# A second raw tile for layer 2's weight conversion, and one place more between the low parts and the products of batch 1's k-q tiles

## The chip, the core and the metric

The kernel runs on one core of one Trainium2 chip. The core has a matrix engine (TensorE, here PE; its weight loads are PEld), two engines for elementwise work and reductions (VectorE, DVE; ScalarE, ACT), a third, slower one (GpSimd, POOL), and SyncE (SP), which in this kernel issues every DMA from one queue in order. Each engine runs its own instructions in order and waits on semaphores for the others. The metric is the time of one execution in microseconds (us) on the device, lower is better.

## What is computed

Three stages follow one another. An attention over channels, with B = 2 batches of N = 6080 rows and C = 256 channels; then two feed-forward layers of width 2048 over the 12160 rows:

```python
qn = q / (np.linalg.norm(q, axis=1, keepdims=True) + 1e-06)
kn = k / (np.linalg.norm(k, axis=1, keepdims=True) + 1e-06)
s = kn.transpose(0, 2, 1) @ qn / tau             # [B, C, C]
a = softmax(s)                                    # over the last axis
x = (v @ a).reshape(12160, 256)

r = np.maximum(x @ w_in, 0.0)                     # layer 1
x = (s * (r * r) + b) @ w_out

h = x @ w2_in                                     # layer 2
x = (h * np.cos(h)) @ w2_out
```

q, k and v come in as float32 and the weights as float64; the kernel reads a float64 as two int32 words and makes a float32 of them itself.

## The kernel before

Every float32 operand of a matmul is split into a high part and a low part (`hi`, `lo`), and every product is three matmuls: high by high, high by low, low by high. The 12160 rows are cut into 12 pairs of blocks (512 columns, and 480 in the last pair of each batch). A **unit** is one pair against one of NJ = 8 slices of the 2048 hidden features; layer 1 is units 0 to 95 (NL = 96) and layer 2 units 96 to 191. From unit 8 on a unit forms its four hidden blocks with seven products instead of eight (a Strassen scheme), which is 21 matmuls of 512 columns at line 294, and then 24 output matmuls at line 419 for the unit before it.

The order of PE, ACT, DVE and POOL is written out by hand in the main loop. The order of a unit on PE is mm1 and mm5; **hook 0**; the first output block (6 matmuls); hook 1; mm6, mm2, the second output block; **hook 2**; mm7, mm3; **hook 4**; the third and fourth output block, mm4; **hook 6**; then hook 7 and the next unit. mm7 (line 294, into `ps_u` or `ps_x`) waits for `add6` (DVE, line 333), which reads what mm6 has written.

Side work is done in small steps that are hung on those hooks: `at(k, h, fn)` puts a function at hook h of unit k, and `steps(generators, places)` advances a generator by one `yield` at each place. A step's instructions stand in each engine's queue at that hook. Two pieces of side work are touched here.

**Batch 1's k-q tiles (`qk1`, lines 633 to 660).** While layer 1 works on batch 0 (units 9 to 38), 48 tiles of 128 rows of q and k are read, and their products are summed for batch 1's attention. The places are hooks 0, 2, 4 and 6 of 30 units, 120 in all. Tile i starts at the place `starts` gives it (line 846): there ACT makes the high parts `qk1h` (line 642) and the squares (line 648). At the next place DVE makes the low parts `qk1l` (line 652) and POOL adds the squares (line 654). At the place after that PE runs six matmuls of 256 columns (line 659), which read `qk1h` and `qk1l`. Both have two buffers, so the high part of tile i + 2 has to wait for the products of tile i.

**Layer 2's weights (`cv2_next`, lines 739 to 763).** From unit 50 on, sixteen blocks of layer 2's float64 weights are converted, alternating between a block `c` of the first matrix and a block `d` of the second (c0, d0, c1, d1, ...). One place is one of the hooks 0, 1, 6, 7. A `c` takes ten places and a `d` six, so that a pair takes four units: c0 and d0 start in units 50 and 52, c1 and d1 in 54 and 56, and so on to c7 and d7 in 78 and 80. A block's conversion (`conv`) reads the tile `raw` in its first three steps (ACT line 98, DVE lines 97, 100 and 103). In the block's fifth step the load of the next block into `raw` is issued (`cv2_load`, line 736). `raw` has one buffer. A `c` then ends in the tiles `ch` and `cl` (7 x 128 floats; ACT line 169, POOL line 171) and a `d` in `wh` and `wl` (2 x 256 floats; ACT line 760, DVE line 762), which `save` (line 455) writes to DRAM; layer 2 fetches them from there. Each of these four has one buffer of its own.

In units 48, 56, 64, 72 and 80, where layer 1 goes over to the next pair, hook 7 also issues the loads of the pair after it (`x_load`, line 249): sixteen DMAs into `xraw`, in the same SP queue as all else.

Of the kernel before, what the change touches and what calls it, by code (L numbers as in the profile page):

```python
# [10 lines left out]
F32R = mybir.dt.float32r  # L11
I32 = mybir.dt.int32
# [4 lines left out]
P = 128  # L17
# [23 lines left out]
def fused_kernel(ctx: ExitStack, tc: tile.TileContext, q, k, v, tau, w_in, w_out, ms, mb, w2_in, w2_out, res):  # L41
    nc = tc.nc
    act, dve, pe, sp, pool = nc.scalar, nc.vector, nc.tensor, nc.sync, nc.gpsimd
# [47 lines left out]
    def conv(raw, cp, res, nx=2):  # L91

        H, L = raw[:, :, :, 1], raw[:, :, :, 0]
        x = cp.tile([P, 2, 2 * P], I32, tag="cx", name="cx", bufs=nx)
        a = cp.tile([P, 2, 2 * P], F32, tag="ca", name="ca", bufs=1)
        f = x.bitcast(F32)
        dve.tensor_scalar(out=x, in0=H, scalar1=3, scalar2=0x3FFFFFFF, op0=ALU.logical_shift_left, op1=ALU.bitwise_and)  # L97
        act.activation(out=a, in_=H, func=AF.Abs)
        yield
        dve.scalar_tensor_tensor(out=x, in0=H, scalar=-(1 << 30), in1=x, op0=ALU.bitwise_and, op1=ALU.bitwise_or)  # L100
        act.activation(out=a, in_=a, func=AF.Abs, bias=-float(1 << 30))
        yield
        dve.scalar_tensor_tensor(out=x, in0=L, scalar=29, in1=x, op0=ALU.logical_shift_right, op1=ALU.bitwise_or)
        yield
        dve.scalar_tensor_tensor(out=f, in0=a, scalar=float(127 << 20), in1=f, op0=ALU.is_le, op1=ALU.mult)
        res.append(f)
        yield

    def in_src(w, j):
        return w[:, 4 * P * j:4 * P * (j + 1)].rearrange("(k p) (f t) -> p k f t", p=P, t=2)  # L110

    def out_src(w, j):
        return w[2 * P * j:2 * P * (j + 1), :].rearrange("(k p) (f t) -> p k f t", p=P, t=2)
# [47 lines left out]
    def combine(Af, hi, lo, o=0):  # L161

        for x, a, b, op in ((4, 0, 3, ALU.add), (6, 1, 0, ALU.subtract)):
            dve.tensor_tensor(out=Af[:, x, :], in0=Af[:, a, :], in1=Af[:, b, :], op=op)
        yield
        for x, a, b, op in ((5, 4, 1, ALU.subtract), (7, 2, 5, ALU.subtract)):
            dve.tensor_tensor(out=Af[:, x, :], in0=Af[:, a, :], in1=Af[:, b, :], op=op)
        yield
        act.copy(out=hi[:, o:7, :], in_=Af[:, 1 + o:8, :])
        yield  # L170
        pool.tensor_tensor(out=lo[:, o:7, :], in0=Af[:, 1 + o:8, :], in1=hi[:, o:7, :].bitcast(F32), op=ALU.subtract)
# [277 lines left out]
    def save(key, hi, lo):  # L449
        w = 1  # L450
        for x in hi.shape[1:]:
            w *= x
        t = dr.tile([2, P, w], F32, tag=f"kp{key[0]}{key[1]}", name="kept")
        for i, x in enumerate((hi, lo)):
            sp.dma_start(out=t[i], in_=x.rearrange("p a b -> p (a b)").bitcast(F32))
        keep[key] = t
# [50 lines left out]
    with tc.tile_pool(name="pro", bufs=2) as pro:  # L507
# [18 lines left out]
        for c, (t0, p, nj) in enumerate(chunks):  # L526
            rk, rq = raw_t.pop(c)
            hi = pro.tile([P, JM, 4, P], F32R, tag="qkh", name="qkh", bufs=HB)
            lo = pro.tile([P, JM, 4, P], F32R, tag="qkl", name="qkl", bufs=HB)
# [86 lines left out]
    nt1 = (N + P - 1) // P  # L616
# [12 lines left out]
    def qk1_load(i):  # L629
        p = st1["pool"]  # L630
        n = min(P, N - i * P)
        r = p.tile([P, 2, C], F32, tag="qk1", name="qk1", bufs=3)
        sp.dma_start(out=r[0:n, 0, :], in_=k[1, i * P:i * P + n, :])
        sp.dma_start(out=r[0:n, 1, :], in_=q[1, i * P:i * P + n, :])
        st1["r", i] = (r, n)

    def qk1(i):
        p = st1["pool"]
        r, n = st1.pop(("r", i))
        hi = p.tile([P, 2, C], F32R, tag="qk1h", name="qk1h", bufs=2)  # L640
        lo = p.tile([P, 2, C], F32R, tag="qk1l", name="qk1l", bufs=2)
        act.copy(out=hi[0:n], in_=r[0:n])
        acc, S = st1["acc"], st1["S"]
        if i == 0:
            act.activation(out=acc, in_=r, func=AF.Square)
        else:
            sq = p.tile([P, 2, C], F32, tag="sq1", name="sq1", bufs=1)
            act.activation(out=sq[0:n], in_=r[0:n], func=AF.Square)
        if i + 2 < nt1:
            qk1_load(i + 2)  # L650
        yield
        dve.tensor_tensor(out=lo[0:n], in0=r[0:n], in1=hi[0:n].bitcast(F32), op=ALU.subtract)
        if i:
            pool.tensor_tensor(out=acc[0:n], in0=acc[0:n], in1=sq[0:n], op=ALU.add)
        yield
        for m in range(2):
            ksl = slice(m * P, (m + 1) * P)
            for a, (w, x) in enumerate(((hi, hi), (hi, lo), (lo, hi))):
                pe.matmul(S[:, m * C:(m + 1) * C], lhsT=w[0:n, 0, ksl], rhs=x[0:n, 1, :],  # L659
                          start=(i == 0 and m == 0 and a == 0), stop=(i == nt1 - 1 and m == 1 and a == 2), skip_group_check=True)  # L660
# [64 lines left out]
    st2 = {}  # L725
    gst = ExitStack()
    cv2 = [x for j in range(NJ) for x in (("c", j, in_src(w2_in, j)), ("d", j, out_src(w2_out, j)))]

    def cv2_open():
        fst.close()  # L730
        st2["pool"] = gst.enter_context(tc.tile_pool(name="cv2", bufs=1, side="right"))
        cv2_load(0)

    def cv2_load(i):
        raw = st2["pool"].tile([P, 2, 2 * P, 2], I32, tag="raw", name="raw", bufs=1)
        sp.dma_start(out=raw, in_=cv2[i][2])
        st2[i] = raw

    def cv2_next(i):
        kind, j, _ = cv2[i]  # L740
        p = st2["pool"]
        res = []
        yield from conv(st2.pop(i), p, res, 1)
        x = res[0]
        if i + 1 < len(cv2):
            cv2_load(i + 1)
        if kind == "c":
            Af = afp.tile([P, 8, P], F32, tag="Af", name="Af", bufs=1)
            xv = x.rearrange("p k (f c) -> p k f c", f=2)
            for m, sl in ((0, slice(1, None, -1)), (1, slice(2, 4))):  # L750
                act.activation(out=Af[:, sl, :], in_=xv[:, m], func=AF.Copy, scale=INV_A)
            yield
            for m, sl in ((0, slice(1, None, -1)), (1, slice(2, 4))):
                dve.scalar_tensor_tensor(out=Af[:, sl, :], in0=xv[:, m], scalar=INV_B, in1=Af[:, sl, :], op0=ALU.mult, op1=ALU.add)
            yield
            hi, lo = [p.tile([P, 7, P], F32R, tag=f"c{h}", name=f"c{h}", bufs=1) for h in "hl"]
            yield from combine(Af, hi, lo)
        else:
            hi, lo = [p.tile([P, 2, 2 * P], F32R, tag=f"w{h}", name=f"w{h}", bufs=1) for h in "hl"]
            act.activation(out=hi, in_=x, func=AF.Copy, scale=TWO_PI)  # L760
            yield
            dve.scalar_tensor_tensor(out=lo, in0=x, scalar=TWO_PI, in1=hi.bitcast(F32), op0=ALU.mult, op1=ALU.subtract)
        save((kind, j), hi, lo)
# [70 lines left out]
    places = [(u, h) for u in range(NJ + 1, NU0 - NJ - 1) for h in (0, 2, 4, 6)]  # L834
    active = []

    def qk1_place(i):
        for g in list(active):
            if next(g, 0) == 0:
                active.remove(g)  # L840
        if i is not None:
            g = qk1(i)
            next(g)
            active.append(g)

    starts = {(len(places) - 4) * i // nt1: i for i in range(nt1)}
    for x, pl in enumerate(places):
        at(*pl, lambda i=starts.get(x): qk1_place(i))
    u = NU0 - NJ - 1
# [1 line left out]
    for j in range(NJ):  # L851
        steps([lazy(fold1, j)], [(NU0 - NJ + 1 + j, h) for h in (0, 1, 3, 4, 6, 7)])
    at(NU0 + 2, 0, cv2_open)
    todo = steps([lazy(cv2_next, i) for i in range(2 * NJ)],
                 [(u, h) for u in range(NU0 + 2, NL - 2) for h in (0, 1, 6, 7)][1:])

# [67 lines left out]
    for k_ in range(NJ, NU + 1):  # L924
        p, j = divmod(k_, NJ)
# [123 lines left out]
```

## Time and profile before

| | |
|---|---|
| median of three runs | 2157.35 us (2155.8 to 2158.29) |
| the profiled execution | 2159.99 us, its span 2158.2 us |
| PE busy | 2106.7 us, 98% of the span |
| PEld, DVE, ACT, POOL busy | 80%, 77%, 73%, 40% |
| mean granted clock of PE | 0.993 of full speed |
| HBM | 57 GB/s over the span |

The span is what lies between the first instruction and the last. Busy shares are means over stages. Most of the idle time of DVE, ACT and POOL is waiting for the others in a chain in which PE hardly ever stops, so the stretches in which PE itself stops are the ones to look for.

### The profile page before, as it was taken

The numbers are of one execution on the slowest core, as the hardware profiler recorded it, in microseconds if no ns is written. First come the engines' busy times: TensorE is split into PE (matmuls) and PEld (weight loads), VectorE is DVE, ScalarE is ACT, GpSimd is POOL, SyncE is SP. The second block draws the span as 40 slices with busy tenths as digits, with TensorE's granted clock in tenths as the row PEclk, the third lists the DMA queues.
The fourth block names the chain that finished last, engine by engine and source line by source line (L and its number), as shares of the span: only waits on it lengthen the run. The fifth ranks groups of instructions, "written<-read, shape, count | busy, mean of one in ns | idle before, by whom it ended". The sixth has DMA issues, their size and how long they took to land.

```text
span 2158.2 us, 28236 instructions
## 1 busy us (share of the span) xinstructions
PE 2106.7 (98%) x9478; PEld 1733.6 (80%) x9478; DVE 1664.8 (77%) x2410; ACT 1577.1 (73%) x2829; POOL 853.8 (40%) x638
## 2 busy tenths in 40 slices
PE   8799999999999999999999999999999999999997
PEld 7587888888788787878888888888888888888886
DVE  7787977777678787878666778778777777777775
ACT  7686766676666665756657888888888888888875
POOL 0003544443243332323223455444544554444544
PEclk9899999999999999999999999999999999999999
DMA  8432131230312313233053011011011011011011
GB/s 251 127 127 69 40 79 41 72 77 13 88 34 71 105 57 86 74 86 85 0 176 122 15 30 35 15 29 34 15 30 34 15 30 31 18 29 26 4 20 19
DMA packets 255523, 124.80 MB, mean 58 GB/s; under 512 B 206736, under 2 KB 221840, under 8 KB 255376
## 3 DMA queue, kind: packets, MB, share of 16 engines
q1 hardware_dynamic: 255376, 122.99, 21.4%
q8 instruction: 74, 1.21, 0.2%
q14 instruction: 73, 0.60, 0.1%
HBM read 82.31 MB, written 40.63 MB: 57 GB/s over the span
## 4 chain that ended last, share of the span: by engine, by line
PE 76%; DVE 6%; ACT 2%; DMA 1%; issue 1%; SPq 0%; POOL 0%; DVEq 0%; ACTq 0%; POOLq 0%
PE ps_y L419 39%; PE ps_s L294 20%; PE ps_u L294 11%; PE ps_x L294 4%; PE ps_x L659 1%; DVE d L380 1%; DVE r L375 1%; DVE gl L406 1%; DMA raw<-in_moe_w_in_dram 1%; DVE cx L97 1%; ACT gh L401 1%; PE ps_x L179 1%; ACT r L363 0%; DVE ps_s L333 0%; DVE d L349 0%
## 5 line engine op out<-in xcount | busy, mean ns | idle before, releaser
L406 POOL TENSOR_TENSOR gl<-r,gh 128x512 fp32r<-128x512 f32 (+1 forms) x560 | 730.1, 1311 | 1087.7 <-ACT gh L401 716.7
L419 PE MATMUL ps_y<-gh,WOh 128*128 128x512 f32 (+1 forms) x1536 | 474.0, 390 | 0.2 <-ACT gh L401 0.2
L419 PE MATMUL ps_y<-gl,WOh 128*128 128x512 f32 (+1 forms) x1536 | 472.3, 389 | 0.7 <-POOL gl L406 0.7
L419 PE MATMUL ps_y<-gh,WOl 128*128 128x512 f32 (+1 forms) x1536 | 472.5, 389 | 0.0
L401 ACT CAST gh<-r 128x512 fp32r<-128x512 f32 (+1 forms) x680 | 416.4, 616 | 7.0 <-DVE r L375 3.7
L419 PEld LDWEIGHTS ps_y<-gl,WOh 128*128 128x128 f32 x1536 | 288.1, 188 | 62.0 <-POOL gl L406 3.1
L419 PEld LDWEIGHTS ps_y<-gh,WOl 128*128 128x128 f32 x1536 | 288.6, 188 | 59.5
L419 PEld LDWEIGHTS ps_y<-gh,WOh 128*128 128x128 f32 x1536 | 286.9, 188 | 59.1 <-ACT gh L401 0.9
L294 PE MATMUL ps_s<-xh,WIh 128*128 128x512 f32 (+1 forms) x778 | 308.4, 396 | 1.1 <-DVE r L375 0.7
L294 PE MATMUL ps_s<-xh,WIl 128*128 128x512 f32 (+1 forms) x778 | 304.3, 391 | 0.6 <-DVE WIl L822 0.6
L294 PE MATMUL ps_s<-xl,WIh 128*128 128x512 f32 (+1 forms) x778 | 303.0, 390 | 0.0
L375 DVE TENSOR_TENSOR r<-r,ps_s 128x512 f32<-128x512 f32 (+1 forms) x374 | 251.5, 672 | 3.6 <-ACT r L363 2.7
L333 DVE TENSOR_TENSOR ps_s<-s,ps_u 128x512 f32<-128x512 f32 (+1 forms) x136 | 93.7, 689 | 198.1 <-ACT r L369 62.2
L396 ACT ACTIVATE r<-r 128x512 f32<-128x512 f32 (+1 forms) x384 | 228.8, 621 | 3.8 <-DVE r L390 3.8
L363 ACT ACTIVATE r<-ps_s 128x512 f32<-128x512 f32 (+1 forms) x197 | 116.7, 593 | 121.5 <-PE ps_s L294 121.1
L294 PEld LDWEIGHTS ps_s<-xh,WIh 128*128 128x128 f32 x778 | 146.5, 188 | 48.8 <-DVE r L375 21.0
L294 PE MATMUL ps_u<-xh,WIh 128*128 128x512 f32 (+1 forms) x431 | 170.3, 395 | 12.9 <-DVE ps_s L333 12.3
L385 ACT ACTIVATE n<-ps_s 128x512 int32<-128x512 f32 (+1 forms) x192 | 114.3, 595 | 84.0 <-PE ps_s L294 83.9
L294 PEld LDWEIGHTS ps_s<-xh,WIl 128*128 128x128 f32 x778 | 146.6, 188 | 31.9 <-DVE WIl L822 1.1
L294 PE MATMUL ps_u<-xl,WIh 128*128 128x512 f32 (+1 forms) x431 | 168.7, 391 | 0.0
L294 PE MATMUL ps_u<-xh,WIl 128*128 128x512 f32 (+1 forms) x431 | 168.4, 391 | 0.0
L294 PEld LDWEIGHTS ps_s<-xl,WIh 128*128 128x128 f32 x778 | 146.8, 189 | 26.2
(167 smaller groups left out, 3282.0 us busy)
## 6 DMA issues: line engine op xcount, KB each, us to landing
xraw<-in_v_dram SPq DMA_DIRECT2D x160, 64.0 KB, 2.6
ys<-dr SPq DMA_DIRECT2D x40, 256.0 KB, 2.5
xraw<-ys SPq DMA_DIRECT2D x40, 256.0 KB, 2.7
out_dram<-dr SPq DMA_DIRECT2D x160, 64.0 KB, 2.0
raw<-in_moe_w_in_dram SPq DMA_DIRECT2D x16, 512.0 KB, 3.7
raw<-in_moe_w_out_dram SPq DMA_DIRECT2D x16, 512.0 KB, 3.6
qk<-in_k_dram SPq DMA_DIRECT2D x47, 128.0 KB, 2.1
qk<-in_q_dram SPq DMA_DIRECT2D x47, 128.0 KB, 2.2
```

Source lines behind the costliest of these rows:

```text
L97: dve.tensor_scalar(out=x, in0=H, scalar1=3, scalar2=0x3FFFFFFF, op0=ALU.logical_shift_left, op1=ALU.bitwise_and)
L179: pe.matmul(pf[:, m * C:(m + 1) * C], lhsT=eT[a][:, e, m * P:(m + 1) * P], rhs=w[:, e, :], start=(n == 0), stop=(n == 5))
L294: pe.matmul(acc[:, 0:n], lhsT=a[:, w, :], rhs=b[:, 0:n], start=(start and s == 0), stop=(stop and s == 2), skip_group_check=True)
L333: dve.tensor_tensor(out=U[k_, "e"][:, 0:n], in0=U[k_, "s5"][:, 0:n], in1=U[k_, "b"][:, 0:n], op=ALU.add)
L363: act.activation(out=r[:, 0:n], in_=U[k_, i][:, 0:n], func=AF.Relu)
L375: dve.tensor_tensor(out=r[:, 0:n], in0=r[:, 0:n], in1=h[:, 0:n], op=ALU.mult)
L380: dve.scalar_tensor_tensor(out=h[:, 0:n], in0=h[:, 0:n], scalar=0.0, in1=h[:, 0:n], op0=ALU.max, op1=ALU.mult)
L385: act.activation(out=q_[:, 0:n], in_=U[k_, i][:, 0:n], func=AF.Copy, bias=0.25)
L396: act.activation(out=r[:, 0:n], in_=r[:, 0:n], func=AF.Sin, bias=HALF_PI, scale=TWO_PI)
L401: act.copy(out=G[k_, i][0][:, 0:n], in_=RR[k_, i][:, 0:n])
L406: eng.tensor_tensor(out=lo[:, 0:n], in0=RR.pop((k_, i))[:, 0:n], in1=hi[:, 0:n].bitcast(F32), op=ALU.subtract)
L419: pe.matmul(accs[p, t][m][:, 0:n], lhsT=wo[w][:, f, m * P:(m + 1) * P], rhs=g[x][:, 0:n], start=(j == 0 and f == 0 and s == 0), stop=(j == ...
```

## The change

```diff
@@ qk1
         if i:
             pool.tensor_tensor(out=acc[0:n], in0=acc[0:n], in1=sq[0:n], op=ALU.add)
         yield
+        yield
         for m in range(2):
@@ cv2_open, cv2_load
         cv2_load(0)
+        cv2_load(1)
 
     def cv2_load(i):
-        raw = st2["pool"].tile([P, 2, 2 * P, 2], I32, tag="raw", name="raw", bufs=1)
+        raw = st2["pool"].tile([P, 2, 2 * P, 2], I32, tag="raw", name="raw", bufs=2)
@@ cv2_next
-        if i + 1 < len(cv2):
-            cv2_load(i + 1)
+        if i + 2 < len(cv2):
+            cv2_load(i + 2)
@@ cv2_next, the branch of a block d
-            hi, lo = [p.tile([P, 2, 2 * P], F32R, tag=f"w{h}", name=f"w{h}", bufs=1) for h in "hl"]
+            hi, lo = [p.tile([P, 2, 2 * P], F32R, tag=f"c{h}", name=f"w{h}", bufs=1) for h in "hl"]
@@ where the places of qk1 are laid out
-    starts = {(len(places) - 4) * i // nt1: i for i in range(nt1)}
+    starts = {(len(places) - 5) * i // nt1: i for i in range(nt1)}
```

The products of a k-q tile move one place back, three places after the tile's start; the starts are spread over 115 places instead of 116. `raw` gets a second buffer, the first two blocks are loaded at the opening, and each block's step then loads the block two further on. In exchange `wh` and `wl` share the one buffer of `ch` and `cl` each (one tag names one set of buffers), which takes 4096 bytes less of each partition, as much as the second `raw` takes.

## Rows read from the trace of the kernel before

**Rows 1.** The page, part 1: busy us, share of the span, instructions.

```profile
PE 2106.7 (98%) x9478; PEld 1733.6 (80%) x9478; DVE 1664.8 (77%) x2410; ACT 1577.1 (73%) x2829; POOL 853.8 (40%) x638
```

**Rows 2.** The chain of work that ended last, by time: start us, us, what.

```profile
661.02 2.72 PE ps_y L419 x12
671.22 2.72 PE ps_y L419 x12
...
702.28 2.72 PE ps_y L419 x12
...
722.68 2.72 PE ps_y L419 x12
...
789.80 2.72 PE ps_y L419 x12
...
810.20 2.72 PE ps_y L419 x12
...
878.55 2.72 PE ps_y L419 x12
...
898.95 2.72 PE ps_y L419 x12
...
966.07 2.72 PE ps_y L419 x12
...
986.47 2.72 PE ps_y L419 x12
...
1007.46 2.72 PE ps_y L419 x12
```

**Rows 3.** Waits, 640 to 1010 us: who waited for whom, us in total, times, longest.

```profile
DVE cx L97 <- DMA raw<-in_moe_w_in_dram: 16.3, 3, 6.3
```

**Rows 4.** Instructions by time: start us, us, what, idle time before with its releaser.

```profile
664.75 0.38 DVE L97 TENSOR_SCALAR cx<-raw 128x512 int32<-128x512 int32 x1
...
754.45 0.43 DVE L97 TENSOR_SCALAR cx<-raw 128x512 int32<-128x512 int32 x1 [5.04 <-DMA raw<-in_moe_w_in_dram]
...
755.53 0.79 PE L294 MATMUL ps_u<-xh,WIh 128*128 128x512 f32 x1 [3.02 <-DVE ps_s L333]
```

**Rows 5.** The same view of SP's queue alone, 700 to 752 us.

```profile
700.04 0.38 SPq L736 DMA_DIRECT2D raw<-in_moe_w_in_dram  x1
...
738.08 0.32 SPq L455 DMA_DIRECT2D kept<-cl  x1
...
738.92 9.59 SPq L249 DMA_DIRECT2D xraw<-in_v_dram  x16
...
749.61 0.41 SPq L736 DMA_DIRECT2D raw<-in_moe_w_in_dram  x1
```

**Rows 6.** Stretches: from:to, length, busy us by engine, clock, DMA share, GB/s.

```profile
755.42:758.83 3.41, 3.29 (x8) 2.62 (x9) 2.30 (x5) 1.92 (x5) 0.00 (x0) 0.50 0.00 0
```

**Rows 7.** Waits, 200 to 530 us.

```profile
PEld ps_x L659 <- DVE qk1l L652: 3.8, 7, 1.4
...
PE ps_x L659 <- DVE qk1l L652: 1.7, 2, 1.0
```

**Rows 8.** Instructions by time, 236 to 239 us, of POOL, DVE and PE.

```profile
236.41 1.73 POOL L654 TENSOR_TENSOR acc1s<-acc1s,sq 128x512 f32<-128x512 f32 x1
...
236.93 1.77 DVE L652 TENSOR_TENSOR qk1l<-qk,qk1h 128x512 fp32r<-128x512 f32 x1
...
237.42 0.28 PE L659 MATMUL ps_x<-qk1h 128*128 128x256 f32 x1
...
238.75 0.39 PE L659 MATMUL ps_x<-qk1l,qk1h 128*128 128x256 f32 x1 [1.05 <-DVE qk1l L652]
238.97 0.28 PE L659 MATMUL ps_x<-qk1h,qk1l 128*128 128x256 f32 x1
239.09 0.28 PE L659 MATMUL ps_x<-qk1h 128*128 128x256 f32 x1
```

**Rows 9.** Instructions by time, 442 to 443 us: the last product, the next high part.

```profile
442.19 0.28 PE L659 MATMUL ps_x<-qk1h,qk1l 128*128 128x256 f32 x1
...
442.79 0.62 ACT L642 CAST qk1h<-qk 128x512 fp32r<-128x512 f32 x1
```

**Rows 10.** DMA issues, 640 to 1010 us: count, KB each, median us to landing.

```profile
kept<-cl SPq DMA_DIRECT2D x8, 448.0 KB, 2.5
```

**Rows 11.** Instructions by time, 747 us: the high part of block d1.

```profile
747.43 0.63 ACT L760 ACTIVATE wh<-cx 128x512 fp32r<-128x512 f32 x1 [2.55 <-DVE cx L105]
```

## The prediction

> **What bounds the kernel now.** I read the busy shares first: PE is busy for 98% of the span and no other engine for over 80% [rows 1], so time is lost only where PE stops or is late, and each such place has to be found. The chain of waits in order of time is the view for that: the pair of output blocks (twelve matmuls, "x12") comes once per unit at a fixed point of PE's order, so its starts are the unit clock. Undisturbed, two follow each other by 10.20 us (661.02 and 671.22) [rows 2]. A unit has 45 matmuls of 512 columns, so one takes 10.20 / 45 = 0.227 us, and there is nothing left between them. What the change touches can therefore be priced directly: as the excess of a stretch over 10.20 us per unit, and, where six 256-column matmuls of a k-q tile are in a unit, as the excess of one of those over the next.
>
> The waits then say who is late. In the stretch from 640 to 1010 us DVE's first conversion step waited three times for the DMA that fills `raw`, 16.3 us in total, longest 6.3 [rows 3]. Of eight blocks `c` these are c2, c4 and c6, in units 58, 66 and 74, two units behind a change of pair. SP's queue shows why: the load of c2 was issued at 749.61, behind sixteen loads of `xraw` that kept SP from 738.92 for 9.59 us; the load of c1, with no change of pair near, left at 700.04 [rows 5]. DVE sat idle for 5.04 us, `add6` stood behind the waiting step in DVE's queue, and PE's mm7 waited 3.02 us for `add6` [rows 4]. When PE restarts, its granted clock is 0.50 for 3.41 us, the 1.2 GHz level, right after the gap, and then full again [rows 6].
>
> **The change part by part.**
>
> The load two blocks ahead. It removes the three waits. Stretch by stretch [rows 2]: from 722.68 to 789.80 are six units, 67.12 us, which is 67.12 - 61.20 = 5.92 over the pace. Part of that is not the load's. A block `d` costs a little wherever it starts: 671.22 to 702.28 is three units with d0 and no late load, 31.06 - 30.60 = 0.46 over. At a change of pair a `d` costs slightly more: 986.47 to 1007.46 is two units with d7 in the second and no block `c` behind it, 20.99 - 20.40 = 0.59 over. The stretch of c2 holds one of each (d1 at the change of pair, d2 alone), so the late load's share is 5.92 - 0.59 - 0.46 = 4.87. From 810.20 to 878.55, the same with c4: 68.35 - 61.20 - 1.05 = 6.10. From 898.95 to 966.07, with c6: 67.12 - 61.20 - 1.05 = 4.87. Sum **15.84 us**. As a cross-check on the first: the gap of 3.02 us and half of the 3.41 us at half clock give 4.73.
>
> Where does it go? The load of c2 will be issued in c1's fifth step, whose buffer is free after c1's third, in units 54 and 55: a unit ahead of the sixteen loads, and three units ahead of its use. Next in line at unit 58 is DVE's own work ahead of `add6`: the low part of d1, a transpose of `xraw` and the first step of c2. The nearest row without a late load is c0 in unit 50, also two units behind a change of pair: its first step ran at 664.75 with no wait [rows 4], and its unit took exactly 10.20 us [rows 2]. It lacks only the low part `wl` of a block before it. So I take zero for what remains. From above I bound it at what a `d` costs, 0.46 us for each of the three, and more loosely at half the present loss, 7.9 us in all; below zero I see no reason for a gain. The loads of blocks `d` move ahead likewise, from a place where they waited for nothing. At the opening a second load of 512 KB goes out right behind the first; d0, which needs it, starts two units after c0. Both are at zero, covered by that distance.
>
> The shared buffer. `wh` of a `d` may now be written only after the save of `cl` of the `c` before it has landed, and `ch` of the next `c` after the save of `wl`. This adds a wait on ACT, where the copies that seed the products are queued behind it and PE's mm6 waits for those. For d1: the save of `cl` was issued at 738.08 [rows 5], such saves land after 2.5 us [rows 10], so at 740.6, and `wh` started at 747.43 [rows 11]. Slack 6.8 us, and this is the tight one of the two, since the next `ch` comes nine places, two units, after `wl`. Cost zero, covered by those 6.8 us; without that cover, see the rivals.
>
> The products one place later. The second view is the waits from 200 to 530 us: PE's weight loads waited 3.8 us in seven places for the low parts, PE itself 1.7 us in two [rows 7]. Both are faces of the same delay. The start-to-start times of the six products tell it fully: normal is 0.12 us (238.97 to 239.09); at 237.42 it was 1.33 and then 0.22, so 1.31 lost [rows 8]. Low parts and products are one place apart, and places are uneven: between hooks 2 and 4, and between 6 and the next 0, stand only six matmuls, 6 x 0.227 = 1.36 us. Here DVE made the low part in 1.77 us from 236.93, while PE wanted it at 237.5. With one place more, at least 6 + 15 = 21 matmuls lie between, 4.77 us, which is more than any low part was late. I take nearly all of it, **3.6 us** (between 1.7 from the one row and 3.8 from the other).
>
> What that adds: the high part of tile i + 2 waits for the products of tile i, which now come a place later. Ten of the tiles start only four places after the last but one, so one place remains, mostly products at hook 4 and the high part at hook 6. In the nearest row such products ended at 442.19 + 0.28 = 442.47 and ACT began a high part at hook 6 at 442.79 [rows 9]: 0.3 us of slack. It is thin, but a short wait on ACT there delays no PE work directly. Zero, at most 0.5 us for each of ten tiles. The spread of the starts (115 for 116) moves some tiles by a place; the number of instructions stays.
>
> One rule speaks against this part. In the row the low part took 1.77 us while POOL's addition ran from 236.41 for 1.73 us [rows 8]. The Trainium skill, "SBUF — State Buffer", section "SBUF: two separate sides", says that VectorE (with two SBUF inputs) and GpSimd share a port pair under an exclusive lock, and that the loser blocks for the whole instruction. The row agrees: 236.41 + 1.73 is 238.14, and the low part ended 0.56 us later. By that rule the change shortens no low part; more of the tiles start at hook 6 now (18 for 12), so more of these blocked low parts stand ahead of `add6`, and the sum would be smaller; I price that as a rival from rows.
>
> **Sum.** 15.84 + 3.6 = 19.4 us. The profiled execution took 2159.99 us, 1.8 more than its span, and becomes 2140.6. It lies 2.64 us above the median of the runs, 2157.35; the same gain from the median gives 2137.95, so **2138 us**, a ratio of 0.991.
>
> **The rivals.**
>
> DVE becomes the bound at the three units. If what stands ahead of `add6` in units 58, 66 and 74 is late without any DMA (the step that reads `raw`, or a low part, blocked by POOL), each costs what a `d` costs today, 0.46: 2138 + 1.4 = 2139.4; the six more low parts at hook 0 at that price add 2.8, 2142.2; and if half of the loss stays, 2138 + 7.9 = 2145.9. For it speaks that a `d` does lose those 0.46 us, against it c0's unit at exactly 10.20. The rule on the shared port pair, in the Trainium skill's "SBUF — State Buffer", is what would bring this case about.
>
> The k-q part gains nothing: ACT's high parts, ten of them, are late by up to 0.5 us and hand that on to PE, 5 us lost for 3.6 gained, 2138 + 5 = 2143. Against it: ACT is busy for 73% of the span and catches up.
>
> The change doesn't do what it says: the order of SP's queue is not written by hand, and if the loads are still put behind the sixteen, only the k-q part is left, 2157.35 - 3.6 = 2153.7. Against it: the buffer is free and the issue stands in the program a unit earlier.
>
> Slower: the save of `cl` falls behind the sixteen loads at the changes of pair (units 56, 64, 72, 80), where it now leaves just 0.84 us ahead of them [rows 5]. It would leave at about 749.5, land at 752.0, and hold ACT at `wh` from 747.43 for 4.6 us, about as long as DVE is held today. ACT stands nearer to PE (mm6's seed), so I price each at the largest of the three losses, 6.10: 4 x 6.10 = 24.4, against 19.4 gained, 2157.35 + 5.0 = 2162.4. It decides from the point where that save lands over 6.8 us later than now. Against it: the save is ready before the loads are due, and leaves ahead of them today.
>
> **How the numbers follow.** Forecast 0.76; DVE at the three units 0.12; the k-q part without gain 0.05; loads still behind 0.04; slower 0.03. The range goes from 2135 (3.8 instead of 3.6, the spread of the runs below their median, 1.6, and as much again for what I don't see) to 2146 (the half-loss case); it holds the first three. Runs of this kernel can tell about 0.2%, 4.3 us, from no change. Below 2153.0 lie the first three, 0.93, of which I give 0.01 to no change; the case at 2153.7 lies within the bound, so no change is 0.05; slower 0.03; faster 0.92.
>
> **What would show it.** In the trace after: the loads of c2, c4 and c6 issued before the sixteen; no wait of DVE's first step for `raw`; no granted clock of 0.50 between 640 and 1010 us; three stretches of six units at 62.2 us; the products never waiting for `qk1l`. Each step is wrong if its mark is missing: a wait of ACT line 760 or 169 for a DMA tells of the shared buffer, a wait of ACT line 642 for PE of the two buffers of `qk1h`, and a mm7 still late without any DMA, of DVE. If the span falls by far less than 19 us with all the marks there, a new wait has come in that I have not named.

## The result, and the profile after

The changed kernel takes 2138.5 us (median of four runs, 2138.25 to 2139.89) against 2157.18 us before (2155.8 to 2158.29): ratio 0.9912, 95% interval 0.9900 to 0.9925. The forecast was 2138.0. The execution profiled after took 2138.25 us.

The page of the changed kernel, part 1 and the clock line of part 2 (the granted clock of PE in 40 slices, in tenths):

```profile
span 2136.5 us, 28243 instructions
...
PE 2098.3 (98%) x9478; PEld 1729.3 (81%) x9478; DVE 1667.9 (78%) x2410; ACT 1576.3 (74%) x2829; POOL 856.2 (40%) x638
...
PEclk9899999999999999999999999999999999999999
```

PE has the same number of instructions and 8.4 us less busy time than in [rows 1]; 5.4 of these lie in units 50 to 83, where before the matmuls at the half clock lasted longer [rows 6].

The chain of work that ended last, by time (start us, us, what), the rows that answer to [rows 2]:

```profile
655.49 2.72 PE ps_y L419 x12
665.69 2.72 PE ps_y L419 x12
...
696.76 2.72 PE ps_y L419 x12
...
717.21 2.72 PE ps_y L419 x12
...
779.47 2.74 PE ps_y L419 x12
...
799.89 2.72 PE ps_y L419 x12
...
862.26 2.72 PE ps_y L419 x12
...
882.71 2.72 PE ps_y L419 x12
...
945.01 2.74 PE ps_y L419 x12
...
965.43 2.72 PE ps_y L419 x12
986.42 2.72 PE ps_y L419 x12
```

(The chain's row of the unit after 965.43 is not among its longest, so the last two are two units apart.) The three stretches of six units take 62.26, 62.37 and 62.30 us, where they took 67.12, 68.35 and 67.12 [rows 2]. The pace is still 10.20 us, and what a block d costs is still there: 31.07 for three units with d0, 20.99 for two with d7.

SP's queue in the changed kernel, the rows that answer to [rows 5]:

```profile
711.59 0.38 SPq L738 DMA_DIRECT2D raw<-in_moe_w_in_dram  x1
...
732.60 0.32 SPq L455 DMA_DIRECT2D kept<-cl  x1
...
733.45 9.84 SPq L249 DMA_DIRECT2D xraw<-in_v_dram  x16
...
744.38 0.40 SPq L738 DMA_DIRECT2D raw<-in_moe_w_out_dram  x1
```

The load of c2 now leaves at 711.59, more than 20 us before the sixteen loads. The one that stands behind them, at 744.38, is that of d2, whose first step on DVE comes 27 us later, at 771.91. DVE in unit 58, instructions by time:

```profile
742.65 0.69 DVE L764 SCALAR_TENSOR_TENSOR wl<-cx,wh 128x512 fp32r<-128x512 f32 x1 [0.75 <-ACT wh L762]
743.26 0.70 DVE L257 STREAM_TRANSPOSE vturn<-xraw 128x512 f32<-128x512 f32 x1
743.89 0.39 DVE L97 TENSOR_SCALAR cx<-raw 128x512 int32<-128x512 int32 x1
745.12 0.70 DVE L333 TENSOR_TENSOR ps_s<-s,ps_u 128x512 f32<-128x512 f32 x1 [0.84 <-PE ps_u L294]
```

The first step of c2 runs without waiting, and `add6` (L333) waits for PE's mm6, not for DVE's own work. Nothing between 640 and 1010 us waits for a DMA into `raw` any more, and the granted clock there is 1.00.

To put the whole difference in its place, each kernel's span can be cut where PE starts mm1 of units 9, 39, 50 and 84. In the changed kernel these are (instructions by time, PE):

```profile
188.51 0.39 PE L294 MATMUL ps_s<-xh,WIh 128*128 128x512 f32 x1
...
532.23 0.39 PE L294 MATMUL ps_s<-xh,WIh 128*128 128x512 f32 x1
...
658.73 0.39 PE L294 MATMUL ps_s<-xh,WIh 128*128 128x512 f32 x1
...
1010.08 0.39 PE L294 MATMUL ps_s<-xh,WIh 128*128 128x512 f32 x1
```

Before, they are 190.46, 537.06, 664.25 and 1031.10. The stretches, with those of the kernels that were run for the next section, in us:

| kernel | units 9 to 38 (k-q tiles) | 39 to 49 | 50 to 83 (weights) |
|---|---|---|---|
| before | 346.61 | 127.19 | 366.85 |
| changed | 343.71 | 126.50 | 351.36 |
| changed, run again (a_again) | 343.51 | 127.23 | 351.21 |
| e1_raw_only | 346.73 | 126.51 | 351.51 |
| e2_qk_only | 343.61 | 126.09 | 365.89 |
| e3_shared_only | 346.61 | 126.59 | 368.37 |
| e5_split_loads | 346.50 | 126.93 | 352.06 |
| e6_late_save | 343.62 | 128.91 | 355.52 |
| e7_two_more | 350.78 | 127.73 | 351.27 |
| e8_d_one_later | 343.56 | 126.53 | 349.25 |
| e9_cl_earlier | 343.55 | 126.42 | 347.18 |
| e10_starts_as_before | 343.75 | 126.77 | 351.43 |

The changed kernel gains 15.49 us in the weights' stretch and 2.90 in the k-q tiles', 18.4 together, and the medians differ by 18.7. The span of the profiled execution shrank by 21.7, but 1.95 of that lie ahead of unit 9, where no edit reaches, and the rest in units 39 to 49 and in layer 2. The k-q column repeats within 0.25 us from kernel to kernel that share that code, so a difference of half a microsecond can be read from it, which a median of whole runs can't give.

### The profile page after: what moved, and what is told of

Same layout as the page of the kernel before. It is cut to its first block, busy times and chain, and to the rows that moved or that the text cites. A ratio compares the mean times of both kernels' runs of the same rounds, so it can differ in the third digit from the quotient of the medians.

```text
span 2136.5 us, 28243 instructions
## 1 busy us (share of the span) xinstructions
PE 2098.3 (98%) x9478; PEld 1729.3 (81%) x9478; DVE 1667.9 (78%) x2410; ACT 1576.3 (74%) x2829; POOL 856.2 (40%) x638
## 4 chain that ended last, share of the span: by engine, by line
PE 88%; DVE 7%; ACT 3%; issue 2%; DMA 1%; SPq 0%; DVEq 0%; POOL 0%; ACTq 0%; POOLq 0%
PE ps_y L419 44%; PE ps_s L294 23%; PE ps_u L294 12%; PE ps_x L294 5%; PE ps_x L660 2%; PE ps_x L179 1%; DVE d L380 1%; DVE r L375 1%; DVE gl L406 1%; DVE cx L97 1%; ACT gh L401 1%; ACT r L363 0%; DVE qkl L537 0%; DVE d L349 0%; ACT ch L169 0%
## 5 line engine op out<-in xcount | busy, mean ns | idle before, releaser
L333 DVE TENSOR_TENSOR ps_s<-s,ps_u 128x512 f32<-128x512 f32 (+1 forms) x136 | 93.8, 689 | 192.8 <-ACT r L369 53.9
```

Of the source, the lines that this page charges most:

```text
L333: dve.tensor_tensor(out=U[k_, "e"][:, 0:n], in0=U[k_, "s5"][:, 0:n], in1=U[k_, "b"][:, 0:n], op=ALU.add)
```

## The experiments

The theory is the prediction's: three loads stood behind sixteen others in SP's queue, and a few products of k-q tiles came too soon after their low parts; the shared buffer costs nothing. The rivals are that the depth of the buffer and not the queue matters, that the shared buffer or the two buffers of `qk1h` bring new waits, and that DVE is late in those units by itself. The parts were first taken one by one.

**The raw tiles and the shared buffer alone** (e1_raw_only): the changed kernel without these two edits.

```diff
-        yield
         yield
         for m in range(2):
-    starts = {(len(places) - 5) * i // nt1: i for i in range(nt1)}
+    starts = {(len(places) - 4) * i // nt1: i for i in range(nt1)}
```

> The changed kernel with the k-q part undone: two raw tiles and the shared buffer alone. By the prediction's sum the three late loads are worth 15.84 us and the shared buffer nothing, so 2157.2 - 15.8 = 2141.4 us, ratio 0.9927. If part of the gain of the whole change came from the two parts together (a stall of one that hid a stall of the other), this and the run of the k-q part alone add up to clearly less than the 18.7 us between the medians of the two kernels.

Measured: 2140.92 us, ratio 0.9915 (0.9902 to 0.9929). Its weights' stretch is 351.51, as in the changed kernel, and its k-q stretch 346.73, as in the kernel before. The waits of the k-q products are all there (waits, 200 to 530 us):

```profile
PEld ps_x L659 <- DVE qk1l L652: 4.0, 8, 1.3
...
PE ps_x L659 <- DVE qk1l L652: 1.7, 2, 1.0
```

**The k-q part alone** (e2_qk_only): the kernel before with the opposite two edits.

> The kernel before with the k-q part alone (one place more, starts over 115 places). The prediction says 3.6 us, so 2153.6, ratio 0.9983. The unit clock of the changed kernel's trace makes it 2.9 (from the start of unit 9 to the start of unit 39 it takes 333.4 us instead of 336.3), so 2154.3. The rival, ACT's high parts late at the two buffers, says no gain: 2157 or above. The three late loads must still be there, 16 us of waits of line 97 for the DMA.

Measured: 2154.84 us, ratio 0.9981 (0.9971 to 0.9990), and the k-q stretch 343.61, 3.0 us below before. The late loads are still there (waits, 640 to 1010 us):

```profile
DVE cx L97 <- DMA raw<-in_moe_w_in_dram: 15.9, 3, 5.8
```

By the stretches the two parts add up: 15.3 and 3.0 alone, 15.5 and 2.9 together. Neither hides the other's stall. By the medians on that chip they gain 17.8 and 3.9, 21.6 together, which is not less than 18.7 either.

**The shared buffer alone** (e3_shared_only): one edit of the kernel before.

```diff
-            hi, lo = [p.tile([P, 2, 2 * P], F32R, tag=f"w{h}", name=f"w{h}", bufs=1) for h in "hl"]
+            hi, lo = [p.tile([P, 2, 2 * P], F32R, tag=f"c{h}", name=f"w{h}", bufs=1) for h in "hl"]
```

> The kernel before with one edit: wh and wl take the buffers of ch and cl, raw stays single. The instructions of every engine and of SP's queue stand in the same order, so only the added wait can change the time. The prediction says nothing, covered by 6.8 us: 2157.2, ratio 1.000. The rival says that the wait bites (a save that lands late at some handovers): above 2158.5, with a wait of ACT line 760 or DVE line 762 for a DMA in the trace.

Measured: 2157.42 us, ratio 0.9992 (0.9983 to 1.0001). Between 640 and 1010 us no instruction waits for a save. The stretch is 1.5 us longer than before, but in the three late loads themselves (waits, 640 to 1010 us), which vary by as much from run to run:

```profile
DVE cx L97 <- DMA raw<-in_moe_w_in_dram: 17.4, 3, 6.6
```

The shared buffer costs nothing that can be measured.

**The queue without the buffer** (e5_split_loads): the kernel before, in which the sixteen loads at four changes of pair are issued as eight and eight, a unit apart.

```diff
-        at(k0, 1 if l2 else 7, lambda p=p: [x_load(p, t, m) for m in range(2) for t in range(2)])
+        if l2 or not NU0 + 8 <= k0 <= NU0 + 32:
+            at(k0, 1 if l2 else 7, lambda p=p: [x_load(p, t, m) for m in range(2) for t in range(2)])
+        else:
+            at(k0, 7, lambda p=p: [x_load(p, t, 0) for t in range(2)])
+            at(k0 + 1, 7, lambda p=p: [x_load(p, t, 1) for t in range(2)])
```

> The kernel before, raw single and with buffers of its own, but the sixteen loads of xraw at the changes of pair of units 56, 64, 72 and 80 are issued as eight at hook 7 of that unit and eight at hook 7 of the next. The load of c2 then stands behind eight loads (4.8 us) and not sixteen, and should leave near 744.5, land near 748.3 and be there when c2 starts at 749.4. If the queue ahead of the load is what made it late, the three stalls go without any second buffer: 2157.2 - 15.8 = 2141.4. If it is the depth of the buffering, or if DVE is late by itself in those units, they stay: 2157.

Measured: 2143.42 us, ratio 0.9927 (0.9914 to 0.9939). SP's queue by time, and DVE's wait for `raw` over 640 to 1010 us:

```profile
737.09 5.68 SPq L249 DMA_DIRECT2D xraw<-in_v_dram  x8
742.87 0.91 SPq L436 DMA_DIRECT2D ys<-dr  x2
743.87 0.42 SPq L736 DMA_DIRECT2D raw<-in_moe_w_in_dram  x1
744.34 5.15 SPq L249 DMA_DIRECT2D xraw<-in_v_dram  x8
```

```profile
DVE cx L97 <- DMA raw<-in_moe_w_in_dram: 3.6, 3, 1.8
```

The load of c2 leaves at 743.87, as expected. With one buffer, no second tile and nothing shared, 14.8 of the 15.5 us are gone. So most of it was the queue. The loads are still a little late (3.6 us of DVE's idle time), which costs PE only the remaining 0.7; the three took 4.40, 6.33 and 5.94 us from issue to landing, where that of c1 took 3.90.

**The slower rival made on purpose** (e6_late_save): the changed kernel with the saves of `ch` and `cl` issued two steps into the next block, so that at a change of pair the save of `cl` is behind the sixteen loads (that of `ch` still leaves ahead of them, at 726.20).

```diff
+        for n_, _ in enumerate(conv(st2.pop(i), p, res, 1)):
+            if n_ == 1 and late:
+                save(*late.pop())
+            yield
-        yield from conv(st2.pop(i), p, res, 1)
...
             yield from combine(Af, hi, lo)
+            late.append(((kind, j), hi, lo))
+            return
```

> The changed kernel, with the saves of ch and cl of each block c issued two steps into the next block d and not at the end of c. At the four changes of pair the save of cl then stands behind the sixteen loads in SP's queue: the slower rival of the prediction, made on purpose. cl's save lands near 747, wh was to start near 742, so ACT waits some 5 us at wh, four times. By the rival's price, the largest of the three late loads each time: 4 x 6.10 = 24.4, so 2138.5 + 24.4 = 2162.9. If ACT's queue has slack that DVE's has not, less than half of that: below 2150. The other four handovers should cost nothing.

Measured: 2143.77 us, ratio 0.9933 (0.9919 to 0.9948), so some 5 us slower than the changed kernel and not 24. The waits over 640 to 1010 us, then SP, DVE and PE by time in unit 58:

```profile
DVE wl L771 <- DMA kept<-cl: 10.6, 3, 4.4
```

```profile
743.46 0.40 SPq L455 DMA_DIRECT2D kept<-cl  x1
...
747.82 1.10 DVE L771 SCALAR_TENSOR_TENSOR wl<-cx,wh 128x512 fp32r<-128x512 f32 x1 [3.70 <-DMA kept<-cl]
...
750.51 0.50 PE L294 MATMUL ps_u<-xh,WIh 128*128 128x512 f32 x1 [1.24 <-DVE ps_s L333]
```

The wait is there, but on DVE at `wl` and not on ACT at `wh`. It comes at all four changes of pair: the view counts three, and in unit 74 it books the wait, 2.92 us, to ACT's `gh`, though the save landed only at 915.78 and `wl` began at 915.90. It begins early in PE's unit, ahead of mm6, and most of it passes before `add6` is wanted: 3.70 us on DVE are 1.24 on PE. Units 58, 66 and 74 take 11.73, 12.06 and 11.05 us instead of 10.20, 4.2 in all, and the fourth wait, in unit 82, which has no block `c`, costs PE nothing. The stretch of units 39 to 49, which no edit touches, was 2.4 longer in this profile than in the changed kernel's; PE's clock was at 0.50 there for 3.41 us.

**One more place** (e7_two_more): the changed kernel with the products four places after the start.

```diff
         yield
         yield
+        yield
         for m in range(2):
-    starts = {(len(places) - 5) * i // nt1: i for i in range(nt1)}
+    starts = {(len(places) - 6) * i // nt1: i for i in range(nt1)}
```

> The changed kernel with the products of a k-q tile yet another place later (four after the start; starts over 114 places). For the tiles whose second successor starts four places later, the high part then waits for products that PE runs at the same place, on purpose: ACT should wait for PE at line 642 about ten times for 0.5 to 1.5 us. The prediction says that such a wait on ACT delays no PE work: 2138.5, within 1 us. The rival says it is handed on: 5 us or more, above 2143.

Measured: 2145.66 us, ratio 0.9940 (0.9923 to 0.9956); the k-q stretch is 7.1 us longer than in the changed kernel and 4.2 longer than before. Waits, 200 to 530 us:

```profile
ACT qk1h L642 <- PE ps_x L661: 28.9, 19, 3.2
...
PEld ps_u L294 <- DVE ps_s L333: 3.1, 4, 1.2
PEld ps_y L419 <- ACT gh L401: 2.6, 2, 1.3
```

The rival is right here. ACT waits for the two buffers of `qk1h` nineteen times, up to 3.2 us, and hands it on: through its own high parts `gh` and through what DVE gets from ACT. In the changed kernel the same line waits for nothing. So one place more is the last that these two buffers give without such waits.

**What a block d costs.** A `d` starts at the end of a unit, at hook 7. In the changed kernel the unit behind it (53, 57 and so on to 81) still takes 10.67 to 10.90 us, and there PE waits for `add6` once for each of the eight blocks (PE's waits, 640 to 1010 us):

```profile
PE ps_u L294 <- DVE ps_s L333: 1.9, 8, 0.4
```

The first step of a `d` on DVE stands at the place right after POOL's `cl`. First, each `d` was started one place later (e8_d_one_later):

```diff
         res = []
+        if kind == "d":
+            yield
         yield from conv(st2.pop(i), p, res, 1)
```

> The changed kernel with each block d starting one place later, so that its first step on DVE no longer stands at the place right after POOL's cl (2.57 us). Each block d costs 0.46 us over the pace at present. If DVE's first step is held by cl on POOL, seven or eight of these go: 2138.5 - 3.5 = 2135. If the cost is the d's own steps, nothing changes: 2138.5. The blocks drift by one place for each pair against the changes of pair, so a load may fall behind the sixteen: then it is slower.

Measured: 2136.32 us, ratio 0.9898 (0.9883 to 0.9913), and the weights' stretch 349.25. It was run once more next to the changed kernel:

> The changed kernel once more, as the measure for the three that are sent with it: 2138.5 us, ratio 0.9912.

> The kernel with each block d one place later once more, next to the changed kernel on the same chip. Its stretch from unit 50 to unit 84 took 2.1 us less than that of the changed kernel (349.25 for 351.36), so the median should be 2 us below it, 2136.5; if its lower time was the chip of that job, they are level.

Measured on one chip: 2139.15 us for the changed kernel (ratio 0.9921, 0.9907 to 0.9934) and 2136.79 for this one (0.9908, 0.9895 to 0.9922); the stretches are 351.21 and 349.27. So 2 us are gained of the 3.5 expected. The blocks drift against the hooks, and some units still cost 0.2 to 0.6: in four of the eight blocks `d` the first step still runs beside an instruction of POOL, and takes 0.9 to 1.7 us. The next kernel (e9_cl_earlier) keeps them in step: `cl` moves to the place of `ch`, and the `d` starts where it did.

```diff
-    def combine(Af, hi, lo, o=0):
+    def combine(Af, hi, lo, o=0, apart=True):
...
         act.copy(out=hi[:, o:7, :], in_=Af[:, 1 + o:8, :])
-        yield
+        if apart:
+            yield
         pool.tensor_tensor(out=lo[:, o:7, :], in0=Af[:, 1 + o:8, :], in1=hi[:, o:7, :].bitcast(F32), op=ALU.subtract)
...
+        if kind == "d":
+            yield
         yield from conv(st2.pop(i), p, res, 1)
...
-            yield from combine(Af, hi, lo)
+            yield from combine(Af, hi, lo, 0, False)
```

> The changed kernel with POOL's cl moved one place ahead, to the place at which ACT makes ch, and with one empty place before each block d. A pair of blocks takes four units again, so nothing drifts against the changes of pair. DVE's first step of d then stands two places behind cl. If cl on POOL is what holds that step, each of the eight blocks d loses its 0.46 us: 2138.5 - 3.7 = 2134.8, and below the kernel whose blocks drift. If cl, at its new place, holds other steps of DVE with two SBUF inputs for as long, nothing is gained: 2138.5.

Measured on the same chip: 2134.72 us (2133.07 to 2135.42), ratio 0.9897 (0.9884 to 0.9911), the fastest of all, 4.4 below the changed kernel's 2139.15 (2138.33 to 2140.99). POOL and DVE at d0 in the changed kernel run again:

```profile
689.42 2.58 POOL L171 TENSOR_TENSOR cl<-Af,ch 128x896 fp32r<-128x896 f32 x1
...
689.94 2.36 DVE L97 TENSOR_SCALAR cx<-raw 128x512 int32<-128x512 int32 x1
```

and POOL and DVE with `cl` a place earlier:

```profile
683.56 2.13 POOL L172 TENSOR_TENSOR cl<-Af,ch 128x896 fp32r<-128x896 f32 x1
...
689.39 0.41 DVE L97 TENSOR_SCALAR cx<-raw 128x512 int32<-128x512 int32 x1
```

The first step of `d` takes 0.41 us when POOL is not in its way, and 2.36 when it starts behind `cl`. PE no longer waits for `add6` in these units. The stretch is 347.18 us, and 34 units at 10.20 are 346.80: only 0.4 us are left over that pace.

**The spread of the starts** (e10_starts_as_before): the changed kernel with 116 for 115.

> The changed kernel with the starts of the k-q tiles spread over 116 places as before, the products one place later. In the changed kernel's trace the k-q stretch (units 9 to 38) gained 2.9 us and not 3.6: PE's weight loads wait longer for POOL's low parts, 2.9 us in nine places for 1.3 in four. If the new spread of the starts (18 tiles at hook 6 for 12) brings POOL's sums next to those low parts, this kernel's stretch is shorter by some 0.7 us, 343.0 for 343.7; if it is the products' move itself, it stays. The median says too little of so small a step: 2138.

Measured: 2139.59 us, ratio 0.9919 (0.9907 to 0.9932), the k-q stretch 343.75. The spread is not the cause of the missing 0.7 us; the reading is in the next section.

## Why the prediction held, point by point

**The late loads.** Predicted 15.84 us; the three stretches of six units gained 4.86, 5.98 and 4.82, 15.66 in all, and units 50 to 83 gained 15.49. Here the unit clock did the work: one row per unit, an undisturbed pace, and two stretches that carried the ordinary costs alone. That nothing would take the place of the late loads in those units was right too: they take 10.20 to 10.25 us. That c0's unit, the same distance behind a change of pair with its data at hand, showed the pace was the row that told this in advance. That the queue was the main cause is shown by e5, which takes nearly all of the stall away without any second buffer. Two things the working left out: in the kernel before, the three loads also took 4.74, 5.64 and 5.29 us from issue to landing, for 3.57 of c1's, which is some 5 of the 16.3 us of DVE's wait; and what a late load costs is not fixed, since it hangs on whether PE's clock falls behind it (in e2 unit 74 took 13.31 us, before 15.04; see the last section). The sum of 19.4 us was 1.0 too high against the stretches, so that 2138 meets the median to half a microsecond is in part luck.

**The products one place later.** Predicted 3.6, measured 2.9 to 3.0. The step itself is right, and no product waits for a low part any more. What was mis-sized is the term's remainder, taken at nothing: PE now waits longer for something else. Waits, 200 to 530 us, of the changed kernel,

```profile
PEld ps_y L419 <- POOL gl L406: 2.9, 9, 0.3
```

and of the kernel before:

```profile
PEld ps_y L419 <- POOL gl L406: 1.3, 4, 0.3
```

Counted from PE's starts over units 9 to 38, delays of over 0.03 us at the products fell from 3.8 to 0.2 us, the predicted 3.6, and those at line 419 rose from 1.0 to 1.75. With the starts as before the second is 1.9 (e10), so it goes with the later products and not with the spread. Why POOL's low parts are the next ones late was not taken further.

**The rule on the shared port pair.** The rival that it would have brought about, low parts at hook 0 that make `add6` late, did not come: in the changed kernel's k-q stretch PE's weight loads wait for line 333 once, 0.2 us. But a hold of DVE by POOL was in the trace in a place that I had counted as the price of a block d, and e9 shows it. `cl` on POOL ends at 689.42 + 2.58 = 692.00, and DVE's step, which needs 0.41 us, ends at 692.30; in all eight blocks `d` it takes 1.63 or 2.36 us and ends 0.3 us behind `cl`. The Trainium skill, "SBUF — State Buffer", section "SBUF: two separate sides", has the loser of that port pair block for the whole of the other's instruction, and these times agree. The Trainium skill names two cases there, a VectorE instruction with two SBUF inputs and one in a mode that takes both of its ports. This step has one SBUF input, so it would have to be the second, and no run here shows in which mode it runs: that `cl` holds it is shown, that it is by this lock is inferred. I had taken the 0.46 us as a fixed price and asked only in a rival what it was made of; that was the 4 us left on the table.

**The shared buffer.** Zero was right (e3), but the working named the wrong wait. I wrote that `wh` waits for the save of `cl`. `wh` has the buffer of `ch`, and `wl` that of `cl`; the tight wait is on DVE at `wl`, as e6 shows. The slack was there either way: in the changed kernel `wl` of d1 started some 10 us after the save of `cl` had left, at 742.65 for 732.60.

**The slower rival's price.** 6.10 us for each place, 24.4 in all; e6 measured 4.2 in the stretch. Two things were wrong. The wait falls on DVE and not on ACT, as said. And I priced a wait by the nearest stall of about the same length, though the late load had held DVE until 754.45, after five microseconds of idle time [rows 4], and then cost the clock as well; the wait for the save began earlier against PE's unit and cost PE 1.24 us, with no loss of clock between 640 and 1010 us. So this rival, as e6 makes it, takes back 4 of the 18 us and does not end on the slower side.

**A wait on ACT at the k-q high parts.** "A short wait on ACT there delays no PE work directly" was too broad. The change brings no such wait, so the sum did not suffer, but e7, in which ACT does wait, lost 7.1 us. The 0.3 us of slack of [rows 9] was the right number to read, and it was enough.

## What to carry to other kernels

Where one engine sets the pace, find a row that comes once per unit of work, take its undisturbed distance, and price every suspected stall as the excess of a stretch over it, with a stretch that has all but the stall as the control: that gave 15.84 us for a measured 15.5. A DMA that comes late may be late in its queue more than on its way: see what is issued ahead of it before adding a buffer, since moving half of those issues did nearly the same here. A recurring small excess that is booked as an ordinary cost should be opened too: the 0.46 us of each block d was one instruction held by another engine, and moving that by one place was worth another 4 us.

## What the runs showed of the hardware

PE's clock did not fall after every gap, and the length of the gap alone does not tell when it falls. In the kernel before, gaps of 2.90 to 4.25 us were each followed by 3.41 us at 0.50 of the clock, the 1.2 GHz level. In e6, PE stopped for 1.24 us at 750.51, and the stretches around it were granted the full clock, 2.4 GHz (from:to, length, PE busy, clock, DMA share, GB/s):

```profile
740.00:750.00 10.00, 9.27 (x41) 1.00 0.82 224
750.00:760.00 10.00, 9.49 (x42) 1.00 0.23 71
```

But in e2 the third late load stopped PE for nearly as long as in the kernel before, and the full clock stayed (PE's instruction behind the gap, by time, and the stretch behind it as above):

```profile
927.21 0.50 PE L294 MATMUL ps_u<-xh,WIh 128*128 128x512 f32 x1 [2.82 <-DVE ps_s L333]
...
927.21:930.60 3.39, 3.39 (x15) 1.00 0.02 5
```

And a gap of 1.75 us that stands in every one of these kernels, ahead of four transposes (near 553 us in the changed kernel), left the clock full in the changed kernel and was followed by the half clock in e10:

```profile
553.04 0.63 PE L702 MATMUL ps_s<-ident,s 128*128 128x128 f32 x4 [1.75 <-DVE r L375]
...
553.00:556.40 3.40, 3.35 (x17) 1.00 0.03 10
```

```profile
553.46 1.08 PE L702 MATMUL ps_s<-ident,s 128*128 128x128 f32 x4 [1.75 <-DVE r L375]
...
553.31:556.72 3.41, 3.26 (x10) 0.50 0.02 4
```

Of thirteen profiles three have the half clock at that place. In these runs a stall of PE therefore costs about its own length and, where the half clock follows, about half of the time that PE works at it, some 1.7 us for 3.41; once, at the second late load of e2, the half clock lasted 6.83 us. What decides whether it follows is not shown here.
